# Loading the values' weights and the bias rows on the ACT queue instead of the SP queue

## The chip, the cores and the metric

The kernel runs on one core of one Trainium2 chip. The metric is the device time of one execution in microseconds (us); the median of several runs is given, and one further execution is profiled.

## The reference

The input x has 2048 rows of 512 columns in bf16. Each row is normalised (layer norm without gain or bias); the result xn feeds two branches, and the output is x plus both.

```python
xn = _layernorm(x, axis=-1)
return x + _A_ref(xn, A_wqkv, A_w_phi, A_wo) + _B_ref(xn, B_w1, B_b1, B_w2)
# A: linear attention, 32 heads of 16
qkv = (x @ wqkv) ...                       # wqkv is 512 x 1536: queries, keys, values
pq, pk = q @ w_phi, k @ w_phi              # a 16 x 16 matrix per head
phi = concat(softmax(p), softmax(-p))      # 32 features, for pq and for pk
kv, z = phi_k^T v, sum(phi_k)
o = (phi_q kv) / (phi_q z + 1e-6);  A = o @ wo
# B: a dense layer of 1792 hidden units
h = x @ w1 + b1;  act = h * tanh(softplus(h));  B = act @ w2
```

## The kernel before, in words

The 2048 rows are 16 tiles of 128 rows, in four groups of four tiles. Everything is held on chip: x as `x_sb`, the turned normalised rows as `xnT`, the hidden activations as `acts`.

The feature matrix w_phi is folded into the key weights (and later into the query weights), so that one product gives pk. For this the kernel loads the key columns of wqkv turned, by two transposing DMAs into the tile `wT` (`load_turned`, L162 to L170; two halves of 256 rows of wqkv), multiplies them with a block-diagonal matrix `Wbd` (`fold`, L172; steps `foldk_0` to `foldk_3`, one for each 128 rows of wqkv, so that `foldk_0` and `foldk_1` need the first half of `wT` and `foldk_2` and `foldk_3` the second), and ScalarE copies the four results into `wkp`, one half of the tile `wkv` (L628). The other half of the tile is `wv`, the value columns of wqkv as they are. So rows of the profile that name `wkv` mean either `wkp` (written on chip) or `wv` (loaded). Most matrix products on either go through `project` (L275).

The opening runs like this. VectorE and ScalarE take the mean and variance of x tiles 0 to 3, one tile at a time (`spread` L198, `total` and `scatter` L203 and L207, `deviate` L219, `invert` L224), normalise each (`apply`, L250), TensorE turns it (`flip`, `turn_pe`, L258), and a copy puts it into `xnT` (`flip=`, L624). Steps `first_i_kt` then multiply quarter kt of tile i with quarter kt of `wkp`: sixteen matmuls in all. On TensorE `foldk_1` and `foldk_0` stand behind the turning of tile 0, then one warming matmul, `foldk_2` and `foldk_3`, and then the turnings of tiles 2, 3 and 1 with the first products between them. Next come `bias` (L634, turns the bias rows `b1b` so that each hidden unit's bias lies in its partition), `value_1` (the first product with `wv`), and, after the rest of this group's keys, the first `unit_0_f` (L290, a slice of the hidden layer from `w1_sb`).

The order of the work is written out by hand: the string PLAN lists steps, and `step` (L594 and on) issues each. Every engine works through its own instructions in that order. Ten matmuls on a tile of ones (`keep_warm`, L582) run on TensorE ahead of the plan.

Loads are issued on two queues. SP, an engine that computes nothing, issues most of them; ACT (ScalarE) issues the first two loads of x and goes on to compute after that. In the order of the code, ScalarE's first instructions behind its DMA issues are a small activation (L566), with the table load that it needs, and then the deviation of tile 0.

The issues before the plan are, on SP: w_phi into `wsrc` (L550), the two halves of `wT` (L167), x tiles 4 to 7 (L554), `b1b` (L555), `wv` (L556), two halves of w1 (L558), x tiles 8 to 11 and 12 to 15 (L560). On ACT: x tile 0, and x tiles 1 to 3 (L552).

Of the kernel before, what the change touches and what calls it, by code (L numbers as in the profile page):

```python
# [85 lines left out]
def kernel(  # L86
# [12 lines left out]
    nc = tc.nc  # L99
    P = 128  # L100
    S, D, NH, DH, F = 2048, 512, 32, 16, 1792
# [10 lines left out]
    wqkv_v = A_wqkv.rearrange("(kt p) c -> p kt c", p=P)  # L112
# [4 lines left out]
    b1_v = B_b1.rearrange("(f p) -> f p", p=P)  # L117
# [25 lines left out]
    b1b = wts.tile([FT, P], BF16, name="b1b")  # L143
    b1f = wts.tile([P, FT], FP32, name="b1f")
    Wbd = wts.tile([P, 4, P], BF16, name="Wbd")
    wkp, wv = wkv[:, 0], wkv[:, 1]
# [15 lines left out]
    def load_turned(base_col, parts=1):  # L162

        wT = lnp.tile([P, 4, 512], BF16, name="wT", tag="xn")
        n = D // parts
        for r in range(0, D, n):
            nc.sync.dma_start_transpose(  # L167
                out=wT[:, :, r : r + n], in_=A_wqkv[r : r + n, base_col : base_col + D]
            )
        return wT  # L170
# [379 lines left out]
        nc.sync.dma_start(wsrc[:], wphi_v)  # L550
    for t in (slice(0, 1), slice(1, 4)):
        nc.scalar.dma_start(x_sb[:, t, :], x_v[:, t, :])  # L552
    held = {"wT": load_turned(D, 2)}
    nc.sync.dma_start(x_sb[:, 4:8, :], x_v[:, 4:8, :])  # L554
    nc.sync.dma_start(b1b[:], b1_v[:, :])  # L555
    nc.sync.dma_start(wv, wqkv_v[:, :, 2 * D : 3 * D])  # L556
    for c in (slice(0, F // 2), slice(F // 2, F)):
        nc.sync.dma_start(w1_sb[:, :, c], w1_v[:, :, c])  # L558
    for t in (8, 12):
# [181 lines left out]
```

## Time and profile before

| what | us |
|---|---|
| median of 3 runs | 175.22 (175.06 to 175.33) |
| the profiled execution | 174.82 |
| its span, first to last instruction | 173.1 |
| TensorE (PE) busy | 167.2 |
| VectorE (DVE) busy | 151.1 |
| ScalarE (ACT) busy | 113.1 |
| GpSimd (POOL) busy | 51.0 |

A row of the timeline has the start in us, the length in us, the engine, the line of the kernel, the operation, what it writes and reads with shapes, the number of instructions merged, and in brackets the idle time before it and what ended that. PEld is TensorE's weight load, which overlaps its matmuls. An engine's name with a q (SPq, ACTq) stands for its instruction stream issuing something, here DMAs. In the DMA view a queue's row gives packets, megabytes, and the share of sixteen engines' time in that window; q1 is SP's queue and q10 is ACT's. A row with "to landing" gives the time from issue to the last byte's arrival. The chain of waits is followed back from the last instruction, or from the end of the window asked for.

### The profile page before, as it was taken

The page shows a single profiled execution, that of the slowest core. Times are in us where ns is not written, and L with a number is a line of the kernel's source. Part 1 is how long each engine was busy: PE and PEld are TensorE (multiplying, and loading weights), DVE is VectorE, ACT ScalarE, POOL GpSimd, SP SyncE. Part 2 cuts the span into 40 slices and gives each one's busy share as a digit, 9 for nine tenths or more (in the row PEclk, how much of TensorE's full clock was granted, in tenths as well). Part 3 has the DMA queues.
Part 4 walks back from the last instruction along what each step waited for, and adds up shares of the span by engine and source line. Part 5 has one row for each costly group of instructions (what it writes and reads, how often), then busy time and mean ns, then how long its engine had stood idle before and what let it go on. Part 6 is the DMA issues. An engine that isn't in the chain of part 4 may idle for free.

```text
span 173.1 us, 2832 instructions
## 1 busy us (share of the span) xinstructions
PE 167.2 (97%) x1021; PEld 82.8 (48%) x1038; DVE 151.1 (87%) x266; ACT 113.1 (65%) x168; POOL 51.0 (29%) x95
## 2 busy tenths in 40 slices
PE   7899999999999999999999999999999999999993
PEld 2544444444455544455455444444444454445571
DVE  2978999999999999999998999999999979886633
ACT  3959999999997999998999998745500401300000
POOL 6021027300450004796006501442380380500000
DMA  5999993827900000000000059217357467657442
GB/s 152 275 350 377 131 299 121 144 100 138 109 0 0 4 0 0 0 2 4 0 0 0 2 124 123 58 23 190 35 114 189 92 165 113 141 129 180 71 141 72
DMA packets 45226, 18.03 MB, mean 104 GB/s; under 512 B 37148, under 2 KB 45212, under 8 KB 45212
## 3 DMA queue, kind: packets, MB, share of 16 engines
q1 hardware_dynamic: 44524, 17.26, 45.0%
q10 hardware_dynamic: 688, 0.59, 1.1%
q8 instruction: 8, 0.13, 0.4%
q14 instruction: 6, 0.05, 0.1%
HBM read 6.84 MB, written 2.10 MB: 52 GB/s over the span
## 4 chain that ended last, share of the span: by engine, by line
PE 72%; DVE 18%; DMA 3%; SPq 3%; issue 3%; DVEq 0%
PE po L525 28%; PE ph L290 17%; PE pproj L275 15%; PE po L534 7%; DMA wkv<-in_A_wqkv_dram 3%; DVE m L361 3%; DVE e L369 3%; DVE stats L198 3%; DVE xn L250 2%; PE pnd L489 2%; PE pkv L452 2%; DVE sums L388 2%; SPq L167 2%; DVE r L434 1%; DVE e L439 1%
## 5 line engine op out<-in xcount | busy, mean ns | idle before, releaser
L290 PE MATMUL ph<-xnT,w_sb 128*128 128x512 bf16 x224 | 51.4, 379 | 0.2
L525 PE MATMUL po<-w_sb,acts 128*128 128x512 bf16 (+1 forms) x233 | 51.4, 366 | 0.3
L378 ACT ACTIVATE e<-e 128x1024 bf16<-128x1024 bf16 x28 | 28.1, 1052 | 25.6 <-DVE e L348 25.3
L392 POOL TENSOR_TENSOR t<-e 128x512 f32<-128x512 bf16 x14 | 18.5, 1324 | 65.0 <-ACT e L378 65.0
L300 ACT ACTIVATE acts<-ph,b1f 128x512 bf16<-128x512 f32 x56 | 35.3, 700 | 1.9 <-PE ph L290 1.6
L290 PEld LDWEIGHTS <-w_sb 128*128 128x128 bf16 x224 | 21.5, 98 | 25.1 <-issue 0.4
L525 PEld LDWEIGHTS <-acts 128*128 128x128 bf16 x238 | 22.5, 98 | 22.9
L275 PE MATMUL pproj<-wkv,xnT 128*128 128x512 bf16 x123 | 29.7, 379 | 0.6 <-DMA wkv<-in_A_wqkv_dram 0.4
L275 PEld LDWEIGHTS <-xnT 128*128 128x128 bf16 x192 | 18.2, 98 | 21.2 <-DMA wkv<-in_A_wqkv_dram 0.4
L392 POOL TENSOR_TENSOR t<-t 128x256 f32<-128x256 f32 (+1 forms) x30 | 16.9, 563 | 2.4
L388 DVE TENSOR_REDUCE sums<-e 128x64 f32<-128x1024 bf16 x14 | 16.7, 1208 | 0.7 <-ACT e L378 0.7
L542 DVE TENSOR_TENSOR x_sb<-po,x_sb 128x512 bf16<-128x512 f32 (+1 forms) x17 | 10.9, 654 | 5.9 <-PE po L534 5.8
L534 PE MATMUL po<-wqk,ob 128*128 128x512 bf16 (+1 forms) x65 | 15.6, 366 | 0.2
L275 PE MATMUL pproj<-wqk,xnT 128*128 128x512 bf16 x60 | 15.1, 379 | 0.2
L198 DVE BATCH_NORM_STATS2 stats<-x_sb 128x6 f32<-128x512 bf16 x15 | 9.7, 681 | 2.2 <-DMA x_sb<-in_A_x_dram 2.1
L505 DVE TENSOR_TENSOR ob<-pnd,r 128x512 bf16<-128x512 f32 x16 | 11.1, 692 | 0.6
L439 DVE TENSOR_TENSOR e<-e,r 128x2048 bf16<-128x2048 bf16 x8 | 9.8, 1226 | 0.3
L534 PEld LDWEIGHTS <-ob 128*128 128x128 bf16 x68 | 6.3, 98 | 5.8
L327 ACT CAST e<-pproj 128x512 bf16<-128x512 f32 x12 | 6.9, 602 | 2.7 <-PE pproj L275 1.3
L504 DVE RECIPROCAL r<-pnd 128x32 f32<-128x32 f32 x16 | 5.6, 353 | 3.0 <-PE pnd L489 2.9
L310 ACT CAST p<-pproj 128x512 bf16<-128x512 f32 x13 | 7.6, 595 | 0.7 <-PE pproj L275 0.7
L489 PEld LDWEIGHTS <-qT 128*128 128x128 bf16 x128 | 6.2, 97 | 3.8 <-issue 0.7
(81 smaller groups left out, 185.1 us busy)
## 6 DMA issues: line engine op xcount, KB each, us to landing
out_dram<-x_sb SPq DMA_DIRECT2D x15, 128.0 KB, 1.9
w_sb<-in_B_w_dram SPq DMA_DIRECT2D x2, 896.0 KB, 8.5
x_sb<-in_A_x_dram SPq DMA_DIRECT2D x3, 512.0 KB, 10.3
w_sb<-in_B_w_dram SPq DMA_DIRECT2D x2, 640.0 KB, 5.9
wkv<-in_A_wqkv_dram SPq DMA_DIRECT2D x1, 512.0 KB, 5.8
w_sb<-in_B_w_dram SPq DMA_DIRECT2D x1, 512.0 KB, 6.6
wqk<-in_A_wo_dram SPq DMA_DIRECT2D x1, 512.0 KB, 4.0
x_sb<-in_A_x_dram ACTq DMA_DIRECT2D x1, 384.0 KB, 3.3
```

The lines of the kernel that those rows point to most:

```text
L198: nc.vector.bn_stats(statistics(t)[0][:, t % TPG, :], x_sb[:, t, :])
L275: nc.tensor.matmul(pp, lhsT=xnT[:, t, kt, :], rhs=w[:, kt, :], start=(kt == 0), stop=(kt == KT - 1),)
L290: nc.tensor.matmul(ph[:], lhsT=w1_sb[:, kt, f * P : (f + 1) * P], rhs=xnT[:, g * TPG : (g + 1) * TPG, kt, :], start=(kt == 0), stop=(kt == ...
L300: nc.scalar.activation(acts[:, f, g * 512 : (g + 1) * 512], ph[:], ACT.Mish, bias=b1f[:, f : f + 1])
L378: nc.scalar.activation(v, v, ACT.Exp)
L388: nc.vector.reduce_sum(out, part, axis=AX.X)
L392: nc.gpsimd.tensor_tensor(out=to[:], in0=part[:, :, 0:n], in1=part[:, :, n : 2 * n], op=ALU.add)
L439: nc.vector.tensor_tensor(out=vv, in0=vv, in1=r2[:, :, None, :].to_broadcast([P, 128, 8, 2]), op=ALU.mult)
L505: nc.vector.tensor_tensor(out=o_t.rearrange("p (u v g d) -> p u v g d", u=2, v=4, g=4), in0=nd[:, :, :, 0:64].rearrange("p u v (g d) -> p ...
L525: nc.tensor.matmul(po[:, c], lhsT=acts[:, f, t * P : (t + 1) * P], rhs=w2_sb[:, f, c], start=(f == 0), stop=False,)
L534: nc.tensor.matmul(po[:, c], lhsT=oT_of[h][:, 2 + t % 2, j * P : (j + 1) * P], rhs=wo_sb[:, j, c], start=False, stop=(j == 3),)
L542: nc.vector.tensor_tensor(out=y, in0=po[:, c], in1=y, op=ALU.add)
```

## The change

`wv` and `b1b` are issued by ACT, directly behind its two loads of x, in the order `wv`, `b1b`. SP no longer issues them; its issues of w1 and of x tiles 8 to 15 follow directly on that of x tiles 4 to 7. Nothing else is changed: the same bytes go to the same places, and the plan is the same.

```diff
     for t in (slice(0, 1), slice(1, 4)):
         nc.scalar.dma_start(x_sb[:, t, :], x_v[:, t, :])
+    nc.scalar.dma_start(wv, wqkv_v[:, :, 2 * D : 3 * D])
+    nc.scalar.dma_start(b1b[:], b1_v[:, :])
     held = {"wT": load_turned(D, 2)}
     nc.sync.dma_start(x_sb[:, 4:8, :], x_v[:, 4:8, :])
-    nc.sync.dma_start(b1b[:], b1_v[:, :])
-    nc.sync.dma_start(wv, wqkv_v[:, :, 2 * D : 3 * D])
     for c in (slice(0, F // 2), slice(F // 2, F)):
         nc.sync.dma_start(w1_sb[:, :, c], w1_v[:, :, c])
```

## The prediction

> **What bounds the kernel now.** I read the page's first part, then the busy time by stretches, the chain of waits, the timeline of the first 14 us, and last the DMA rows in short windows. First the page, then the stretches (start and end, length, busy time and instruction count of each engine, clock, DMA share, GB/s).
>
> ```profile
> span 173.1 us, 2832 instructions
> PE 167.2 (97%) x1021; PEld 82.8 (48%) x1038; DVE 151.1 (87%) x266; ACT 113.1 (65%) x168; POOL 51.0 (29%) x95
> ```
>
> ```profile
> 0.00:14.00 14.00, 11.97 (x69) 5.58 (x71) 8.93 (x29) 9.02 (x20) 4.77 (x18) 1.00 0.89 269
> 14.00:47.11 33.11, 32.90 (x158) 15.05 (x159) 32.43 (x59) 32.32 (x47) 7.66 (x14) 1.00 0.82 174
> 47.11:80.00 32.89, 32.69 (x229) 16.79 (x232) 31.68 (x45) 31.30 (x45) 14.11 (x26) 1.00 0.00 1
> ```
>
> After 14 us TensorE is busy for 32.90 of 33.11 us and 32.69 of 32.89 us, with VectorE nearly as full. Behind that point no hole is left that could swallow a late start, so I take what is lost or won before 14 us to reach the end one for one. The change acts only in the first 14 us, where the chain of waits reads (start, length, what):
>
> ```profile
> 1.32 1.33 SPq L167
> ...
> 2.71 1.60 SPq L167
> ...
> 4.97 0.54 SPq L555
> ...
> 5.55 5.80 DMA wkv<-in_A_wqkv_dram
> ...
> 11.40 2.56 PE pproj L275 x11
> ...
> 55.49 3.45 PE ph L290 x16
> ```
>
> The last link before dense TensorE work is the values' weights wv (a part of the tile wkv): issued at 5.55 us, landed at 11.35. But the chain shows only what came last there. The timeline shows what the first 11 us wait for:
>
> ```profile
> 0.80 0.91 ACTq L552 DMA_DIRECT2D x_sb<-in_A_x_dram  x2
> 1.73 1.28 ACT L566 ACT_TABLE_LOAD   x1 [1.73 <-PEq L725]
> 3.03 0.20 ACT L566 ACTIVATE root<-eps 128x1 f32<-128x1 f32 x1
> 4.09 0.29 ACT L219 ACTIVATE rstd<-mv,eps 128x1 f32<-128x1 f32 x1 [0.86 <-DVE mv L214]
> 4.42 0.16 DVE L224 RECIPROCAL rstd<-rstd 128x1 f32<-128x1 f32 x1 [0.36 <-ACT rstd L219]
> 4.55 0.63 ACT L203 ACTIVATE junk<-x_sb 128x512 bf16<-128x512 bf16 x1 [0.17 <-DMA x_sb<-in_A_x_dram]
> 5.55 0.40 SPq L556 DMA_DIRECT2D wkv<-in_A_wqkv_dram  x1
> 5.62 0.23 PEld L258 LDWEIGHTS <-xn 128*128 128x128 bf16 x4 [0.96 <-DVE xn L250]
> 5.80 0.49 PEld L175 LDWEIGHTS <-wT 128*128 128x128 bf16 x8
> 6.79 0.45 PEld L175 LDWEIGHTS <-wT 128*128 128x128 bf16 x8 [0.44 <-DMA wT<-in_A_wqkv_dram]
> 7.68 0.42 DVE L624 COPY xnT<-ptr 128x512 bf16<-128x512 bf16 x1 [0.21 <-PE ptr L258]
> 9.24 0.58 ACT L624 COPY xnT<-ptr 128x512 bf16<-128x512 bf16 x1 [0.51 <-PE ptr L258]
> 10.86 0.18 PE L634 MATMUL pb<-ident,b1b 14*128 14x14 bf16 x1
> 11.40 2.55 PE L275 MATMUL pproj<-wkv,xnT 128*128 128x512 bf16 x11 [0.36 <-DMA wkv<-in_A_wqkv_dram]
> 13.65 2.39 PEld L290 LDWEIGHTS <-w_sb 128*128 128x128 bf16 x12 [0.20 <-DMA w_sb<-in_B_w_dram]
> ```
>
> TensorE's weight loads wait 0.44 us for the second half of wT, the transposed key weights (6.79 us). Behind it in TensorE's order stands the turning of x tile 2; VectorE waits 0.21 us for that (7.68), and ScalarE 0.51 us for the next turning (9.24). So a late wT moves everything up to 10.9 us, link by link. Only then comes the wait for wv: TensorE idle 0.36 us at 11.40.
>
> The landing row of wT (least, median, most) goes with its two issues of 1.32 and 2.71 us:
>
> ```profile
> DMA to landing us min/median/max: 4.0/4.2/4.4
> ```
>
> The second half cannot take 4.4 (7.11 us is after 6.79), so it takes 4.0 and lands at 6.71, and the first at 1.32 + 4.4 = 5.72. The first weight load from wT is at 5.80, the first from the second half at 6.79. Both halves are used 0.08 us after landing: neither has slack.
>
> **What the DMA engines do meanwhile.** Windows of the DMA view, in order: 1.8 to 4.1 us (queue rows), 3.4 to 3.8, 3.8 to 3.9, 3.9 to 4.0 (with its queue rows), 4.2 to 4.6, 5.0 to 5.4, 6.2 to 6.6. q1 is SP's queue, q10 ACT's.
>
> ```profile
> q10 hardware_dynamic: 544, 0.52, 73.3%
> q1 hardware_dynamic: 743, 0.07, 23.4%
> ...
> DMA packets 156, 0.16 MB, mean 388 GB/s; under 512 B 5, under 2 KB 156, under 8 KB 156
> ...
> DMA packets 50, 0.03 MB, mean 318 GB/s; under 512 B 24, under 2 KB 50, under 8 KB 50
> ...
> DMA packets 94, 0.03 MB, mean 279 GB/s; under 512 B 86, under 2 KB 94, under 8 KB 94
> q1 hardware_dynamic: 77, 0.02, 86.6%
> q10 hardware_dynamic: 17, 0.01, 28.1%
> ...
> DMA packets 447, 0.11 MB, mean 286 GB/s; under 512 B 447, under 2 KB 447, under 8 KB 447
> ...
> DMA packets 315, 0.08 MB, mean 202 GB/s; under 512 B 315, under 2 KB 315, under 8 KB 315
> ...
> DMA packets 67, 0.07 MB, mean 164 GB/s; under 512 B 3, under 2 KB 67, under 8 KB 67
> ```
>
> Until 4.1 us ACT's queue brings x tiles 0 to 3 (0.52 MB); x alone moves at 388 GB/s. wT starts at 3.8 us, and from 4.1 us it has the engines to itself, at 286 and later 202 GB/s, until its last small packets at 6.2 us. Those 2.1 us are what the change fills with another transfer.
>
> **The change part by part.**
>
> *wv goes to ACT's queue.* Its issue would run at about 1.75 us, behind x's two. Its 0.524 MB (512 rows x 512 columns x 2 bytes) stand behind x in the same queue, so x is not delayed, and they begin when x ends, at 4.1 us: beside wT, ahead of everything else on SP's queue. wT is also 0.524 MB; SP's queue had moved 0.07 MB by 4.1 us, 0.016 of it the w_phi load, so 0.05 MB of wT; 0.47 MB is left. For a mixture of the two queues the trace has 318 and 279 GB/s; I take their mean, 0.30 MB per us. Both together then take (0.47 + 0.524) / 0.30 = 3.3 us and end at 7.4 us, instead of 6.2 for wT alone: the second half lands 1.2 us later. Bounds: at the 388 GB/s of x alone it is 2.56 us, 0.5 us later; if wT by itself is slow for a reason of its own (202 GB/s with nobody beside it) and wv fits in the holes, 0; wv wholly ahead, 1.7 us (the rival below). I take 1.2, since the mixed rows are nearest. For the first half: 0.262 - 0.05 = 0.21 MB, alone 0.21 / 0.286 = 0.73 us; with half of 0.30 it takes 1.4, so 0.7 us later. That is less than the second half's 1.2, which decides. Delay of the path up to 10.9 us: 1.2 us.
>
> *The wait for wv goes.* wv ends with wT at about 7.4 us, long before its use, now near 12. Gain: the 0.36 us of TensorE idle at 11.40. Late next is the first half of w1: the weight load at 13.65 waits 0.20 us for it, and its landing row, with an issue at 5.99, is
>
> ```profile
> DMA to landing us min/median/max: 7.6/8.5/9.4
> ```
>
> so 13.59 us. Ahead of w1 go the same bytes as before, so I leave it there; TensorE comes 0.8 us later and finds it landed. Were the path not delayed, that wait would grow again by what was won, unless w1 too came earlier.
>
> *ACT issues two more.* By SP's own issues 0.40 (wv) and 0.54 (b1b) plus two gaps of 0.04: 1.02 us. Queued behind on ACT: the table load, from 1.73 to 2.75; the root that warms it, 4.05 to 4.25; then the first deviation, waited for by VectorE, from 4.09 to 4.27, so 0.18 late. The first turning at 5.62 becomes 5.80, still before wT's first half (now about 6.4), and the sum over tile 3, which waits for x until 4.55, starts at 4.56. Cost nothing, covered by the late wT; 0.18 us if that cover is gone.
>
> *SP issues two fewer.* x tiles 4 to 7 keep their place; the two w1 loads and x tiles 8 to 15 are issued 1.02 us earlier, but wait in the queue behind x tiles 4 to 7, which wait behind wT. Nothing, either way. *b1b* is 3.5 KB behind wv, needed at 10.86: nothing.
>
> Sum: +1.2 - 0.36 = +0.8 us. The profiled execution took 174.82 us, 1.72 more than its span; it would take 175.6. The median of the three runs, 175.22, lies 0.40 above it, and so the predicted median is 176.0.
>
> The Trainium skill ("DMA: Bandwidth & Descriptors", "Issuing engines are not separate DMA queues") says that transfers from all issuing engines end on the same 16 DMA engines and interleave; so by it another queue buys only issue time. The mixed window agrees: with both queues active the total fell to 279 GB/s from x's 388.
>
> **The rivals.**
>
> *wv goes ahead of wT.* If the engines take one packet of each queue in turn, a 1 KB row of wv (153 packets carried 0.15 MB of such rows) goes with each 0.25 KB packet of wT (447 for 0.11 MB). All of wv would be through with only 0.131 MB of wT: 0.655 / 0.30 = 2.2 us, then 0.08 / 0.286 = 0.3 us for the rest of the first half, 2.5 instead of 0.73. The path is then delayed by the first half, 1.7 us: +1.7 - 0.36 = +1.3, 176.6 us. Against it: from 3.9 to 4.0 us q1 had 77 packets to q10's 17, about equal bytes. The Trainium skill ("DMA: Bandwidth & Descriptors", "Queues, rings and completion order") says that each engine goes round-robin between queues, a packet at a time, and counts several descriptors to a packet; taken as equal counts that is this rival's time, and the 77 to 17 do not bear it out.
>
> *Faster: wT is not touched.* If wT is held by its own making of descriptors (its two issues take 1.33 and 1.60 us, and the rate falls to 202 GB/s with nobody beside it), wv fits beside it, and TensorE wins 0.36 us, less up to 0.18 for the late deviation: 174.85 to 175.05 us. It decides while wT's second half is under 0.36 us late. Against it: 286 GB/s at 4.2 us is as much as the mixed windows carry.
>
> *A small delay.* At 388 GB/s for both, +0.46 - 0.36 = +0.1: 175.3 us, no change. For it: x alone shows that rate; against: no mixed window does.
>
> *The clock.* The ten warming matmuls issue 0.42 us apart, against 3.45 / 16 = 0.216 us for the same shape later:
>
> ```profile
> 2.38 0.15 PEld L582 LDWEIGHTS <-ones 128*128 128x128 bf16 x1 [0.28 <-issue]
> 2.80 0.15 PEld L582 LDWEIGHTS <-ones 128*128 128x128 bf16 x1 [0.28 <-issue]
> ```
>
> If the longer wait sends TensorE back to the slow pace, the 16 key matmuls up to 10.9 us cost up to 0.2 us more each, 3.3 us: up to 179.3. Against it: TensorE still has the turning and the folds to do in between. The Trainium skill ("TensorE: Matmul & The Clock Gate", "Part 1: The HAM clock gate") has the clock fall back only after an idle window of about 3.4 us; no row here shows such a fall.
>
> **How the numbers follow.** Forecast (wT 0.8 to 1.5 us late, so 175.65 to 176.4): 0.45. wv ahead: 0.17. Untouched: 0.18. Small delay: 0.14. Clock: 0.06. About 0.2% (0.35 us) is what a measurement of this kernel can tell from no change. Slower: forecast, wv ahead and clock, 0.68. Same: the small delay and 0.03 of the untouched case, 0.17. Faster: 0.15. The range goes from the untouched case's full gain to wv wholly ahead, 174.85 to 176.7; it leaves out the clock and some of both edges.
>
> **What would show it.** Right: wT's landings grow to about 5.1 and 5.2 us after issue; the weight loads from wT wait about 1 us in all; q10 carries some 1070 packets (its 544, 512 rows of wv, 14 of b1b) before 8 us; TensorE waits nowhere for wkv from wv; the dense stretch starts 0.8 us later. Wrong: wT's landings stay at 4.0 to 4.4 (faster), or the first half lands later than 7 us (wv ahead), or warming pace reappears among the key matmuls. It would also be wrong if VectorE or TensorE caught up behind 14 us, which their busy shares there deny.

## The result: slower by 2.7%

The changed kernel takes 179.75 us (median of 4 runs, 179.03 to 180.55); the kernel before, run beside it, takes 175.14 (175.03 to 175.33). The ratio is 1.0273, with a 95% interval of 1.0244 to 1.0302. The profiled execution took 179.03 us, with a span of 177.3 against 173.1. A run more than 1.5% above the fastest of its kernel is left out of every median, range and ratio below, and is named where a profile is of it.

The timeline of the changed kernel, with the lines that answer to those of before (start, length, what; in brackets the idle time ahead):

```profile
1.74 0.51 ACTq L553 DMA_DIRECT2D wkv<-in_A_wqkv_dram  x1
2.28 0.89 ACTq L554 DMA_DIRECT2D b1b<-in_B_b_dram  x1
3.20 1.28 ACT L566 ACT_TABLE_LOAD   x1 [3.20 <-issue]
4.60 0.28 ACT L219 ACTIVATE rstd<-mv,eps 128x1 f32<-128x1 f32 x1
5.14 3.49 SPq L558 DMA_DIRECT2D w_sb<-in_B_w_dram  x2
6.04 0.23 PEld L258 LDWEIGHTS <-xn 128*128 128x128 bf16 x4 [1.38 <-DVE xn L250]
8.68 1.45 SPq L560 DMA_DIRECT2D x_sb<-in_A_x_dram  x2
9.16 0.77 PEld L175 LDWEIGHTS <-wT 128*128 128x128 bf16 x8 [2.90 <-DMA wT<-in_A_wqkv_dram]
10.42 0.79 PEld L175 LDWEIGHTS <-wT 128*128 128x128 bf16 x7 [0.28 <-issue]
15.49 0.18 PE L634 MATMUL pb<-ident,b1b 14*128 14x14 bf16 x1
15.60 2.55 PE L275 MATMUL pproj<-wkv,xnT 128*128 128x512 bf16 x11
17.99 2.75 PE L290 MATMUL ph<-xnT,w_sb 128*128 128x512 bf16 x12
```

Before the change the first hidden matmul stood here:

```profile
13.78 2.75 PE L290 MATMUL ph<-xnT,w_sb 128*128 128x512 bf16 x12
```

The first weight load from wT stands at 9.16 us instead of 5.80: 3.36 us later, of them 2.90 of plain waiting. From there to the bias matmul takes 6.33 us (9.16 to 15.49) instead of 5.06 (5.80 to 10.86): 1.27 more. From the bias to the first product with wv takes 0.11 instead of 0.54, since that product waits for nothing now: 0.43 won. Together 4.20 us, and the first hidden matmul comes at 17.99 instead of 13.78, 4.21 later. The whole span grew by 4.2. So all of it happens before that matmul, and nothing behind it gave any of it back.

The landing row of wT in the changed kernel:

```profile
DMA to landing us min/median/max: 7.1/7.5/7.8
```

With issues at 1.32 and 2.69 and the weight loads at 9.16 and after, the first half lands at 9.12 (7.8 us) and the second at 9.8 (7.1 us): 3.4 and 3.1 us late. The DMA view from 4.2 to 6.2 us, before the change, where wT is alone but for the first of x tiles 4 to 7 (35 of the packets):

```profile
DMA packets 1818, 0.48 MB, mean 238 GB/s; under 512 B 1783, under 2 KB 1818, under 8 KB 1818
q1 hardware_dynamic: 1818, 0.48, 123.1%
```

and with the change, from 4.2 to 6.2 and from 6.2 to 8.0, where wv stands beside it on ACT's queue (q10):

```profile
DMA packets 889, 0.43 MB, mean 215 GB/s; under 512 B 625, under 2 KB 889, under 8 KB 889
q10 hardware_dynamic: 266, 0.27, 67.5%
q1 hardware_dynamic: 623, 0.16, 50.3%
...
DMA packets 851, 0.38 MB, mean 212 GB/s; under 512 B 620, under 2 KB 851, under 8 KB 851
q1 hardware_dynamic: 584, 0.14, 115.6%
q10 hardware_dynamic: 267, 0.24, 48.0%
```

With two loads in flight the engines move less than with wT alone (215 against 238 GB/s), and much less than the 388 of x alone. SP's queue falls from 0.48 MB to 0.16 in the same two microseconds.

The busy time by stretches of the changed kernel shows the second loss. The sixth figure, ahead of the DMA share, is the granted clock:

```profile
8.00:10.00 2.00, 0.83 (x9) 0.84 (x10) 0.00 (x0) 0.00 (x0) 0.00 (x0) 0.80 0.95 234
10.00:12.00 2.00, 2.00 (x16) 1.58 (x15) 0.05 (x1) 1.76 (x5) 0.00 (x0) 0.50 1.07 378
12.00:14.00 2.00, 2.00 (x15) 1.27 (x14) 1.96 (x6) 0.60 (x2) 0.00 (x0) 0.85 1.05 406
```

TensorE's clock fell to half at about 9.2 us (0.80 over two microseconds is 1.2 us at full and 0.8 at half), and came back at about 12.6.

### The profile page after: what moved, and what is told of

Same layout as the page of the kernel before. It is cut to its first block, busy times and chain, and to the rows that moved or that the text cites. A ratio compares the mean times of both kernels' runs of the same rounds, so it can differ in the third digit from the quotient of the medians.

```text
span 177.3 us, 2830 instructions
## 1 busy us (share of the span) xinstructions
PE 169.0 (95%) x1021; PEld 84.1 (47%) x1038; DVE 151.0 (85%) x266; ACT 112.9 (64%) x168; POOL 51.0 (29%) x95
## 4 chain that ended last, share of the span: by engine, by line
PE 68%; DVE 17%; DMA 5%; SPq 5%; issue 2%; DVEq 0%
PE po L525 27%; PE ph L290 16%; PE pproj L275 13%; PE po L534 7%; DMA x_sb<-in_A_x_dram 5%; DVE m L361 3%; DVE e L369 3%; DVE stats L198 3%; DVE xn L250 2%; PE pnd L489 2%; PE pkv L452 2%; SPq L558 2%; DVE sums L388 2%; SPq L167 2%; DVE r L434 1%
```

## The experiments

Each is the kernel before with one edit, unless it says otherwise. "wT late" is the first weight load from wT against the 5.80 us of before.

### Only the values' weights on ACT

```diff
+    nc.scalar.dma_start(wv, wqkv_v[:, :, 2 * D : 3 * D])   # behind x, on ACT
-    nc.sync.dma_start(wv, wqkv_v[:, :, 2 * D : 3 * D])
```

> Only the values' weights go to ACT behind x; the bias rows stay on SP. Theory A (an ordinary load in flight beside the two transposing loads of wT slows both): wT lands as late as with the whole change, 7 to 8 us after issue, and the time is 179.0 to 180.0 us. Rival B (ACT's own issues, 0.51 for wv and 0.89 for b1b, which push the table load from 1.73 to 3.20, carry much of the loss): the larger of the two issues is gone, so at least 0.5 us is won back against the whole change, 178.5 or less.

Measured: 178.65 us (178.29 to 180.62; ratio 1.0214, 1.0192 to 1.0236). In the profile, which is of the run of 180.62, wT is 3.7 us late; landing takes 7.5 to 8.1 us. The bias rows' issue on ACT is gone, and the loss is nearly all still there. The median lies 0.35 us below theory A's range and 0.15 above rival B's bound. The harm sits in wv's load; whether the bias rows on ACT add some tenths to it, these runs do not settle: the ratio of 1.0214 lies clearly under the 1.0273 of the change, but its interval meets that of the changed kernel's second measurement (1.0226 to 1.0281, below).

### Only the bias rows on ACT

```diff
+    nc.scalar.dma_start(b1b[:], b1_v[:, :])   # behind x, on ACT
-    nc.sync.dma_start(b1b[:], b1_v[:, :])
```

> Only the bias rows (3.5 KB) go to ACT; the values' weights stay on SP. Theory A: nothing large stands beside wT, it lands 4.0 to 4.4 us after issue as before; ACT is 0.9 us late with its table load and up to 0.4 us with the first deviation: 174.9 to 175.7 us. Rival B: 176 us or more.

> The version with only the bias rows on ACT, once more: 174.3 to 174.6 us, 0.2 to 0.5% under the kernel before, if its first result holds; 174.7 us or more if that was chance.

Measured: 174.40 us (174.28 to 174.70; ratio 0.9964, 0.9946 to 0.9982), and on another occasion 174.46 (174.25 to 175.19; 0.9976, 0.9961 to 0.9990). The first is below both expectations, the second holds it: this half of the change is a small gain, and this version beats both kernels. Its timeline:

```profile
1.74 0.73 ACTq L553 DMA_DIRECT2D b1b<-in_B_b_dram  x1
4.15 0.29 ACT L219 ACTIVATE rstd<-mv,eps 128x1 f32<-128x1 f32 x1 [0.16 <-DVE mv L214]
5.01 0.50 SPq L556 DMA_DIRECT2D wkv<-in_A_wqkv_dram  x1
6.66 0.45 PEld L175 LDWEIGHTS <-wT 128*128 128x128 bf16 x8 [0.23 <-DMA wT<-in_A_wqkv_dram]
10.96 2.55 PE L275 MATMUL pproj<-wkv,xnT 128*128 128x512 bf16 x11
13.35 2.75 PE L290 MATMUL ph<-xnT,w_sb 128*128 128x512 bf16 x12
```

wv is issued at 5.01 instead of 5.55 and lands 5.3 us later, at 10.3 instead of 11.35. The product with wv starts at 10.96 instead of 11.40 and waits for nothing, and the first hidden matmul comes 0.43 us earlier (13.35 against 13.78); the span is 172.7 against 173.1. ACT's issue of 0.73 us costs 0.06 at the first deviation (4.15 against 4.09).

### The bias rows behind the values' weights, all on SP

```diff
-    nc.sync.dma_start(b1b[:], b1_v[:, :])
     nc.sync.dma_start(wv, wqkv_v[:, :, 2 * D : 3 * D])
+    nc.sync.dma_start(b1b[:], b1_v[:, :])
```

> Everything stays on SP, but the bias rows are issued behind the values' weights instead of ahead of them. Theory F (the 14 short rows in front hold the values' weights up, by their issue of 0.54 us and in the queue): the values' weights land 0.5 to 1.1 us earlier, as when the bias rows went to ACT, and TensorE's 0.36 us wait for them goes: 174.4 to 174.8 us. Rival G (they hold up whatever stands behind them on SP's queue, now w1): 174.9 to 175.3 us, with a longer wait for w1 at 13.65 us.

Measured: 174.79 us (174.31 to 175.02; ratio 0.9993, 0.9979 to 1.0007): no difference that can be told, at the upper end of theory F's range. wv is issued at 5.06 and lands at 10.7, and TensorE waits for neither wv nor w1, so the mechanism of theory F is seen in the trace. The gain is not seen in the time. The profiled run is the longest of the twelve (175.02). In it the turnings at 5.74 us and the first folds went at half pace (0.89 us for the first eight weight loads, against 0.49), and the stretch from the first fold to the bias took 5.46 us instead of 5.06, which is about what the wait for wv had cost. Whether the half pace has to do with this edit, and whether the other eleven runs had it, is not known. It stays inconclusive.

### Half and a quarter of the values' weights on ACT

```diff
+    nc.scalar.dma_start(wv[:, 0:2], wqkv_v[:, 0:2, 2 * D : 3 * D])   # half; a quarter: 0:1
-    nc.sync.dma_start(wv, wqkv_v[:, :, 2 * D : 3 * D])
+    nc.sync.dma_start(wv[:, 2:4], wqkv_v[:, 2:4, 2 * D : 3 * D])     # a quarter: 1:4
```

> Half of the values' weights (two of the four row blocks, 0.26 MB) go to ACT behind x, the other half stays in its old place on SP. Theory A: the two queues share for half as long, so wT's halves land about 1.7 us late instead of 3.4 and 3.1, and TensorE's clock does not fall: 176.2 to 177.3 us. Rival C (it is the fall of TensorE's clock, once TensorE waits at all, that makes the loss): the granted clock falls here too, 178 us or more.

> One of the four row blocks of the values' weights (0.13 MB) goes to ACT behind x, the other three stay in the old place on SP. Theory A with a harm that grows with the bytes: wT lands 0.6 to 1.2 us late and TensorE's clock holds: 175.3 to 176.5 us. Rival J (a collision costs a fixed 2 us or more, however small the load, as the half of the values' weights suggested): 177 us or more.

Measured: the half, 177.93 us (176.82 to 178.43; ratio 1.0158, 1.0112 to 1.0203); the quarter, 177.30 (177.28 to 177.65; 1.0139, 1.0118 to 1.0161). The profile of the half is of its longest run, 179.48, in which wT was 3.4 us late; that is an upper end. The quarter made wT 1.7 us late. Both medians are above the ranges of theory A. By its time the quarter meets rival J's bound, though with wT 1.7 us late and not 2 or more. The half ends just short of rival C's 178 us, and the granted clock does not decide that rival: in the half's runs it was 0.988 to 1.00, with 1.00 for the one of 176.82, which lies in theory A's range; in the quarter's it was 0.987 to 1.00, and the run at 1.00 (177.28) was no faster than those at 0.988 and 0.987 (177.29 and 177.31). The harm grows with the bytes, but not in proportion: a quarter of the bytes brings about half of the time lost. The quarter's weight loads on TensorE read:

```profile
7.53 0.77 PEld L175 LDWEIGHTS <-wT 128*128 128x128 bf16 x8 [1.19 <-DMA wT<-in_A_wqkv_dram]
8.26 0.15 PEld L583 LDWEIGHTS <-ones 128*128 128x128 bf16 x1
8.37 0.15 PEld L175 LDWEIGHTS <-wT 128*128 128x128 bf16 x1
8.79 0.79 PEld L175 LDWEIGHTS <-wT 128*128 128x128 bf16 x7 [0.28 <-issue]
```

From the load for a 512-column warming matmul to the next load that must wait for it passes 0.42 us (8.37 to 8.79), the slow pace, while the granted clock of this profile is 1.00 throughout. So TensorE is at half pace here too, without the clock row saying so. It was so already at 6.00 us, ahead of the wait (0.61 us for the turning of tile 0, against 0.40 before the change), so this half pace is not shown to come from the late wT. The stretch from the first fold to the bias takes 6.10 us (7.53 to 13.63) instead of 5.06, which is 1.0 us of the quarter's loss.

### Another load of the same size beside wT

```diff
+    nc.scalar.dma_start(x_sb[:, 8:12, :], x_v[:, 8:12, :])   # behind x tiles 1 to 3, on ACT
-    for t in (8, 12):
-        nc.sync.dma_start(x_sb[:, t : t + 4, :], x_v[:, t : t + 4, :])
+    nc.sync.dma_start(x_sb[:, 12:16, :], x_v[:, 12:16, :])
```

> The values' weights and bias rows stay on SP; instead x tiles 8 to 11 (0.52 MB in 1 KB rows, as wv, but from another tensor) are loaded on ACT behind x tiles 1 to 3. Theory A (any ordinary load does it): wT lands 7 to 8 us after issue, 179.0 to 180.5 us. Rival D (wv and wT are read from the same rows of one tensor in HBM, and that is what slows them): wT lands under 6 us after issue, 177 us or less.

Measured: 179.43 us (178.67 to 180.50; ratio 1.0259, 1.0213 to 1.0305), wT 3.6 us late, landing after 7.4 to 8.1 us. Rival D falls: the harm does not need wv and wT to be read from the same rows. The DMA view of this kernel from 4.2 to 6.2 us reads like that of the change:

```profile
DMA packets 785, 0.36 MB, mean 179 GB/s; under 512 B 580, under 2 KB 785, under 8 KB 785
q1 hardware_dynamic: 578, 0.15, 62.3%
q10 hardware_dynamic: 207, 0.21, 55.0%
```

### Two queues at once, but without wT

```diff
-    nc.sync.dma_start(wv, wqkv_v[:, :, 2 * D : 3 * D])
         elif kind == "scatter":
             scatter(*n)
+            nc.scalar.dma_start(wv, wqkv_v[:, :, 2 * D : 3 * D])
```

> The values' weights are issued by ACT, but only behind its squares of x tile 3 (near 6.1 us), so that they move from about 7 us on, when wT is through, beside x tiles 4 to 7 on SP; the bias rows stay on SP. Theory A (only a load beside the transposing ones does harm): wT lands 4.0 to 4.4 us after issue, two ordinary loads share the engines without loss, ACT's copies are 0.4 us later: 174.8 to 175.9 us. Rival E (two queues at once are slow whatever they carry): 176.5 us or more.

Measured: 175.07 us (nine runs, 174.34 to 176.82; ratio 1.0026, 0.9998 to 1.0054); a tenth took 179.66. ACT issued earlier than I had reckoned, at 5.35 us, beside its square of tile 3 and not behind it; wv still moved from 7 us on. In the profiled run, the fastest of ten, wT landed after 4.0 to 4.4 us as before. The DMA view of that run from 7 to 8, 8 to 9 and 9 to 10 us:

```profile
DMA packets 331, 0.31 MB, mean 309 GB/s; under 512 B 32, under 2 KB 331, under 8 KB 331
q1 hardware_dynamic: 246, 0.22, 69.4%
q10 hardware_dynamic: 85, 0.09, 29.6%
...
DMA packets 341, 0.35 MB, mean 346 GB/s; under 512 B 12, under 2 KB 341, under 8 KB 341
...
DMA packets 247, 0.33 MB, mean 331 GB/s; under 512 B 9, under 2 KB 247, under 8 KB 247
```

Two ordinary loads share the engines at 309 to 346 GB/s; before the change SP's queue alone moved 349, 347 and 293 GB/s in the same three windows, so the sum is the same. Rival E falls: two queues are not slow in themselves; an ordinary load beside wT is. No run has an ordinary load of 0.25 KB packets in wT's place, so whether it is the transposing or the small packets that makes wT so sensitive is not shown. The spread of the ten runs is far wider than before's; why some took up to 176.8 us stays open, since only the fastest was profiled. The one of 179.66 had a granted clock of 0.99, as runs with a late wT have; whether wv met wT there is not known.

### The size of the rows beside wT

The same volume beside wT in longer and in shorter rows: a row block of w1 in 3.5 KB rows, and the left half of x tiles 8 to 15 in 0.5 KB rows.

```diff
+    nc.scalar.dma_start(w1_sb[:, 0:1, :], w1_v[:, 0:1, :])               # 3.5 KB rows
+    nc.scalar.dma_start(x_sb[:, 8:16, 0:256], x_v[:, 8:16, 0:256])       # the other: 0.5 KB rows
     # the rest of w1, or the right half of x tiles 8 to 15, stays on SP
```

> The values' weights and bias rows stay on SP; beside wT stands instead one of the four row blocks of w1 on ACT behind x (0.46 MB, about as much as wv, but in 128 rows of 3.5 KB instead of 512 of 1 KB). Theory H (the two queues take packets in turn, so what counts is how many packets the ordinary load has): wT lands at most 1.5 us late, 176.0 to 177.5 us. Rival I (the two loads slow each other for as long as both have bytes to move, whatever the packets): wT lands 2.5 to 3.5 us late, 178 us or more.

> Beside wT stands, on ACT behind x tiles 0 to 3, the left half of x tiles 8 to 15: 0.52 MB as before, but in 1024 rows of 0.5 KB; the right half stays on SP, as do the values' weights and bias rows. Theory K (a long ordinary packet holds the transposing load up for longer than its share, so that at equal bytes 3.5 KB rows made wT 7 us late and 1 KB rows 3.4): 0.5 KB rows make it 1 to 2.5 us late, and the time is 176 to 178 us. Rival L (the number of packets counts, and 3.5 KB rows were late for another reason): 4 us late or more, 179.5 us or more.

Measured: 3.5 KB rows, 181.58 us (181.03 to 181.88; ratio 1.0373, 1.0347 to 1.0398); 0.5 KB rows, 178.68 (178.31 to 179.50; 1.0226, 1.0180 to 1.0272). The profile of the first is of its longest run, 183.86, with wT 6.9 us late, an upper end; in that of the second it is 2.7 late. The DMA views from 4.2 to 6.2 us, first the 3.5 KB rows,

```profile
DMA packets 208, 0.12 MB, mean 62 GB/s; under 512 B 187, under 2 KB 187, under 8 KB 208
q10 hardware_dynamic: 21, 0.08, 86.6%
q1 hardware_dynamic: 187, 0.05, 45.2%
```

then the 0.5 KB rows:

```profile
DMA packets 1068, 0.39 MB, mean 194 GB/s; under 512 B 623, under 2 KB 1068, under 8 KB 1068
q10 hardware_dynamic: 445, 0.23, 69.7%
q1 hardware_dynamic: 623, 0.16, 55.7%
```

Theory H falls: fewer, longer packets did the most harm, and beside 21 of them wT got 187 packets through. Rival I's time is met, but wT is 6.9 us late and not 2.5 to 3.5. Not all of that kernel's loss is wT's: in its profile the stretch from the first fold to the bias took 7.48 us (12.74 to 20.22) at the fallen clock, instead of 5.06. Theory K has the direction; 0.5 KB rows were slower than its range and differ little from 1 KB rows (2.7 us late against 3.4), and rival L's 4 us and 179.5 us were not reached. The loads compared come from different tensors, so the length of the rows is not quite all that differs. What makes a transposing load so sensitive to a long packet beside it stays open.

### The changed kernel with TensorE kept busy

```diff
-spread_1 foldk_1 ...
+spread_1 warm warm warm warm warm warm warm warm warm warm warm warm foldk_1 ...
```

> The changed kernel once more, beside the next three on the same chip: 178.5 to 180.5 us, by its earlier runs. Both theories expect the same here.

> The changed kernel with twelve more warming matmuls ahead of foldk_1, where TensorE waits for wT (6.4 to 9.2 us in the profile after). Theory (the fall of TensorE's clock is a loss of its own, on top of the late wT): the granted clock stays at 1.00, the stretch from the first fold to the bias matmul takes about 5.1 us as before the change instead of 6.3, and the time falls by 1.0 to 1.5 us against the changed kernel beside it. Rival (ScalarE's copies set the pace of that stretch whatever the clock): less than 0.4 us is won.

Measured: the changed kernel again, 179.19 us (178.91 to 180.05; ratio to before 1.0253, 1.0226 to 1.0281); with the twelve warming matmuls 177.38 (177.29 to 177.49; 1.0142, 1.0121 to 1.0162). 1.8 us are won by adding work. In its profile, weight loads and stretches:

```profile
6.20 2.31 PEld L582 LDWEIGHTS <-ones 128*128 128x128 bf16 x12
8.63 0.65 PEld L175 LDWEIGHTS <-wT 128*128 128x128 bf16 x8
13.76 0.09 PEld L634 LDWEIGHTS <-b1b 14*128 14x128 bf16 x1 [0.42 <-issue]
```

```profile
8.00:10.00 2.00, 2.00 (x23) 1.41 (x22) 0.00 (x0) 0.51 (x2) 0.00 (x0) 1.00 1.11 314
10.00:12.00 2.00, 1.96 (x21) 1.13 (x19) 1.58 (x5) 1.73 (x5) 0.00 (x0) 1.00 1.06 397
```

The clock holds at 1.00, and the stretch from the first fold to the bias takes 5.13 us (8.63 to 13.76), as before the change, against 6.46 in the control's profile (9.06 to 15.52): 1.33 us by the clock. The rest of the 1.8 is wT, whose first weight load came 0.43 us earlier in this profile than in the control's (8.63 against 9.06), within the spread of such runs. The rival falls.

The control's profile also shows how to take the chain of waits. In the first profile of the changed kernel the chain runs through a load of x tiles 12 to 15 that ended 0.05 us ahead of a VectorE instruction at 18.80, though VectorE was busy until then with the copy that starts at 18.19. In the control it runs where the time is:

```profile
1.32 7.70 DMA wT<-in_A_wqkv_dram
9.02 0.05 issue
9.06 0.62 PE pfold L175 x8
```

## Why the prediction was wrong

The sign, the place and the chain of causes were right; the size was not: +0.8 us forecast, +4.6 measured, and outside the range. Two of the prediction's own signs of being wrong showed: the first half of wT landed later than 7 us (9.12), and the warming pace came back among the key matmuls.

**What bounds the start.** Right. wT has no slack, its lateness moves everything up to the bias matmul, and what is lost there reaches the end: 4.21 us at the first hidden matmul, 4.2 in the span.

**wv beside wT: the step that failed.** The term (0.47 + 0.524) / 0.30 took the rate of the mixture from two windows of 0.1 us, in which x was just ending and wT just starting. That start is not what follows. With the change the mixture begins near the assumed rate and falls; the windows of 4.2 to 4.6 and of 5.0 to 5.4 us read:

```profile
DMA packets 310, 0.11 MB, mean 264 GB/s; under 512 B 276, under 2 KB 310, under 8 KB 310
...
DMA packets 130, 0.08 MB, mean 191 GB/s; under 512 B 74, under 2 KB 130, under 8 KB 130
```

The rate over the real mixture was 0.43 MB in 2.0 us, 0.215 MB per us; it was 0.14 in the control's profile of the same kernel, 0.18 with another load of the same rows, and 0.06 with long rows. I had thought of the engines as a fixed rate to be shared out; with both loads in flight they moved no more in total than wT alone had moved in the same two windows (286 and 202 GB/s, the prediction's rows). And wT got the smaller part: 0.16 of 0.43 MB, where I had counted on half. That makes the first half 3.4 us late (0.7 forecast) and the second 3.1 (1.2 forecast). The rival in which wv goes ahead had the right shape, with the first half deciding, but not the rule (2.3 packets of wT to one of wv, not one to one) and the same wrong rate; it gave 1.7. The Trainium skill ("Advanced Engine Details and Errata", "X-Bar Transpose (TRN2)") calls transposing transfers as fast as ordinary ones. Alone this one moved 202 to 286 GB/s in windows of 0.4 us against x's 388, so the trace does not agree, and nothing there prices the two together.

That x ahead of wv on ACT's queue is not delayed held in the change's own profile (x tiles 1 to 3 landed 3.4 us after issue, 3.3 before), but not in all: it was 4.1 with wv alone, 4.2 with x tiles 8 to 11, 5.0 with the half and 5.5 with the 3.5 KB rows.

**The clock.** I gave it 0.06 and up to 3.3 us. It happened, and it costs 1.3 us: the stretch from the first fold to the bias, 6.33 against 5.06 us, and 5.13 with TensorE kept busy. Where the clock fell earlier it cost more: with wv alone on ACT it fell at 8.6 us, and the stretch took 7.56 us. It had a chance of its own only because I took the waiting to be about 1 us; once wT is 3 us late, it belongs to the same case. The Trainium skill ("TensorE: Matmul & The Clock Gate", "Part 1: The HAM clock gate") has the clock fall after an idle window of about 3.4 us. Here TensorE was idle for 2.73 us at a stretch (9.17 less 6.44), and in the 3.4 us ahead of the fall at 9.2 it had worked 0.40 us. In the control's profile the clock fell only at 9.95, 0.9 us after work had begun again, and with the 0.5 KB rows at 8.12, after an idle stretch of 2.17 us. So 3.4 us without any work were not needed; what was, these runs do not show.

**The wait for wv.** Right: it is gone, 0.43 us between the bias and the product with wv against 0.36 forecast.

**ACT's two issues.** Sized too low: 0.51 and 0.89 us, not 0.40 and 0.54, and the first deviation starts at 4.60, not 4.27. The cover held, since the first turning at 6.04 is still far ahead of wT.

**SP's two issues fewer.** I put the w1 and x loads 1.02 us earlier in issue, at no effect. Only w1's issue began earlier (5.14 against 5.99), but SP's two issues of w1 took 3.49 us instead of 1.06, and the issue of x tiles 8 to 15 moved from 7.10 to 8.68. Nothing waited for them.

**b1b.** "Nothing" was wrong, on its own: moved alone, it wins 0.4 to 0.6 us. In the trace wv is then issued 0.54 us earlier, since the issue of the bias rows no longer stands ahead of it on SP, and lands 1.05 us earlier; what the short rows in the queue add is not separated. Together with wv the gain does not show: the change (179.75 and 179.19) is no faster than wv alone on ACT (178.65).

## What to carry to other kernels

Before a load is moved to a second queue, look at what will be in flight beside it: next to this transposing load an ordinary one cost more than its bytes, and long rows cost most, while two ordinary loads shared without loss. If the transposing load is what the first matmuls wait for, nothing should stand beside it, and small loads that are in the way of others are the ones to move. When a wait of some 3 us opens on TensorE, reckon with the clock too; filling the wait with matmuls that nobody needs won 1.3 us by the clock here.

## What was not expected of the hardware

- With an ordinary load beside it, the transposing load fell from 1783 packets (those under 512 B) in 2 us to 623 with 1 KB rows and to 187 with 3.5 KB rows.
- The time of one DMA issue is not fixed. For wv it was 0.51 us on ACT beside wT's issue and 0.38 on ACT at 5.35 us, and 0.39 to 0.51 on SP. For the bias rows it was 0.89 on ACT (0.73 with the bias rows alone there), and on SP 0.54 before the change but 1.76 with wv on ACT and 3.16 with the 3.5 KB rows there.
- The granted clock in the rows can read 1.00 while TensorE works at half pace, as with the quarter of wv (0.42 us from one 512-column matmul's weight load to the next).
